# The low-word matmuls of a 64-token rest: 64 rows each, two accumulations on two row halves

## The chip, the core and the metric

The kernel runs on one core of one Trainium2 chip. The metric is device time in microseconds for one execution. Time before: 358.18 us, the median of 3 runs (357.99 to 358.22).

## The reference

Attention with product features, then a gated feed-forward block whose gate mixes over tokens. Batch 4, 4 heads of 32 (so 128 channels), 1088 tokens, d_ff 1024:

```python
q_p, k_p = phi(q), phi(k)                       # outer products of S1 x and S2 x
num = q_p @ (k_p.T @ v);  den = q_p @ sum(k_p) + 1e-6
x = num / den                                    # 1088 x 128 for each batch
h = gelu(x @ w_in);  u, v = h[..., :512], h[..., 512:]
v_n = (v - mean(v)) / sqrt(var(v) + 1e-6) * g_ln
v_s = einsum('ts,bsd->btd', w_sg, v_n) + b_sg[None, :, None]
out = x + (u * v_s) @ w_out
```

The einsum over s is the heavy part: 1088 x 1088 by 1088 x 512 for each of 4 batches.

## The kernel before, in words

**Two words for one number.** Matmul operands are split into a high word in the type fp32r (a rounded float that TensorE takes in one pass) and a low word, the difference to the original. A product is three matmuls: high by high, low by high, high by low.

**The token sum.** For one batch, the class `Gate` computes v_s transposed: 4 blocks `db` of 128 channels (NB) by 3 chunks `ci` of about 362 output tokens (CH; CHL in the last batch: 376, 376, 336). One `db` and `ci` is a *unit*: one accumulation z in a PSUM bank, over 9 tiles `t` of 128 input tokens. 1088 = 8 x 128 + 64, so the last tile, t = 8, holds a rest of 64 tokens. For t = 0 to 7, `spatial_h` issues vh x w_h (L378) and vl x w_h (L380), and `spatial_l` issues vh x w_l (L386). For t = 8, the 64 rest tokens stand twice in the 128 rows: rows 64 to 127 of vn, of w_h and of x repeat rows 0 to 63. `split` writes the high word of the rest into rows 0 to 63 of vh[:, 8] and its low word into rows 64 to 127 (L371), so one matmul at L378 does both products with w_h. The third, at L386, takes all 128 rows too; rows 64 to 127 of w_l[8] are zero (L950), so that the low word drops out. It ends the accumulation (stop).

**Around a unit.** `unit` makes u: three matmuls L395 to L397 into pu and a gelu on ScalarE (L400). After the accumulation, `scale` reads z on VectorE (L407) and frees its bank, and `gate` multiplies by u (L430) and splits the product into gh (ScalarE, L433) and gl (VectorE, L434). The gated chunk goes on a list `pend`; `flush`, at t = 7 of a later unit, issues its three output matmuls into po (L463 to L465). z comes from the pool `psn`, which has two banks; the attention sum pkv (L200) takes its turn there as well.

**Batch 0** is different: block 0 is summed in plain fp32 at L937, 9 tiles by 3 chunks, with t = 8 over 64 rows, and block 1 (`first == 1` in `main`) runs its three chunks side by side, all high words first and then all low words. Blocks 2 and 3 of batch 0, and all blocks of batches 1 to 3, go unit by unit. That makes 45 accumulations with a low-word matmul at t = 8.

**Order of the work.** While `Gate.main` of one batch runs, `tick` issues steps of the next batch's attention and first projections (`Side`, with the hand-tuned due times FIRST and LATER). The head is in a fixed order; after it, a scheduler orders each engine's instructions, and `high_priority` pulls scale, gelu and gate forward.

Of the kernel before, what the change touches and what calls it, by code (L numbers as in the profile page):

```python
# [18 lines left out]
P = 128  # L19
# [69 lines left out]
def tile_kernel(ctx: ExitStack, tc: tile.TileContext, qd, kd, vd, sd, wd, bd, wind, gd, woutd, identd, outd):  # L89
# [84 lines left out]
    class Attention:  # L174
# [69 lines left out]
        def qp2(self, j):  # L244
            ci, p = divmod(j, 2)
            cw = CH[ci][1]
            a, b = (x[:, p, :cw] for x in self.e[ci])
            V.tensor_mul(a, a, b)
            qph, qpl = self.qp[j] = [self.pool([P, 512], "r", f"qp{i}{self.b}_{j}", F32R)[:, :cw] for i in "hl"]
            A.copy(qph, a)  # L250
            G.tensor_sub(qpl, a, f32(qph))

        def q3(self, ci):
            c0, cw = CH[ci]
            den = self.pool([P, 512], "r", f"den{self.b}_{ci}")[:, :cw]
            pn = []
            for p in range(2):
                qp = self.qp.pop(2 * ci + p)
                pd = bank(f"pnd{self.b}_{ci}_{p}")[:, :cw]
                kv = [k[:, P * p : P * p + P] for k in self.kvs]  # L260
                mm(pd, lhsT=kv[0], rhs=qp[0], start=True, stop=False)
                mm(pd, lhsT=kv[1], rhs=qp[0], start=False, stop=False)
                mm(pd, lhsT=kv[0], rhs=qp[1], start=False, stop=True)
                yield
                pn.append(pd)
                do = slice(64 * (1 - p), 64 * (1 - p) + 64)
                A.activation(den[64 * p : 64 * p + 64], pd[do], AF.Identity, bias=eps_t[do], scale=1.0)  # L267
                yield
            x = self.pool([P, 512], "r", f"x{self.b}_{ci}")[:, :cw]
            V.reciprocal(den, den)  # L270
            yield
            for p in range(2):
                r = slice(64 * p, 64 * p + 64)
                V.tensor_mul(x[r], pn[p][r], den[r])
            yield
            cs = slice(c0, c0 + cw)
            xh, xl = self.x
            A.copy(xh[:, cs], x)
            yield
            V.tensor_sub(xl[:, cs], x, f32(xh[:, cs]))  # L280
            if ci == len(CH) - 1:
                for t in self.x:
                    V.tensor_copy(t[:, S:SP], f32(t[:, S - 64 : S]))

    class Gate:
# [68 lines left out]
        def split(self, db, t0, n):  # L354

            if db not in self.parts:
                vh = self.pool([P, NT, P], "vh", f"vh{self.b}_{db}", F32R)
                vl = self.pool([P, NT - 1, P], "vl", f"vl{self.b}_{db}", F32R)
                self.parts[db] = vh, vl
            vh, vl = self.parts[db]  # L360
            ts = slice(t0, t0 + n)
            vs = self.vn[:, :, P * db : P * db + P]
            A.copy(vh[:, ts], vs[:, ts])  # L363
            yield
            last = t0 + n == NT
            ts = slice(t0, t0 + n - last)
            if n > last:
                self.last = V.tensor_sub(vl[:, ts], vs[:, ts], f32(vh[:, ts]))  # L368
            if last:

                self.last = V.tensor_sub(vh[64:128, NT - 1], vs[64:128, NT - 1], f32(vh[64:128, NT - 1]))  # L371

        def spatial_h(self, z, db, ci, t):

            vh, vl = self.parts[db]
            c0, cw = self.ch[ci]
            cs = slice(c0, c0 + cw)
            last = mm(z, lhsT=vh[:, t], rhs=w_h[:, t, cs], start=(t == 0), stop=False)  # L378
            if t < NT - 1:
                last = mm(z, lhsT=vl[:, t], rhs=w_h[:, t, cs], start=False, stop=False)  # L380
            return last

        def spatial_l(self, z, db, ci, t):

            c0, cw = self.ch[ci]
            mm(z, lhsT=self.parts[db][0][:, t], rhs=w_l[t][:, c0 : c0 + cw], start=False, stop=(t == NT - 1))  # L386

        def unit(self, pool, db, ci):

# [47 lines left out]
        def end(self, db, ci):  # L437

            self.final = db, ci
            xh, xl = self.x  # L440
            self.wf = self.pool([P, C], "wf", "wout_f")
            V.tensor_add(self.wf, f32(wout_h[:, db]), f32(wout_l[:, db]))
            self.xs = []
            for c0, cw in self.ch:
                self.xs.append(self.pool([P, 512], "r", f"x_f{c0}")[:, :cw])
                V.tensor_add(self.xs[-1], f32(xh[:, c0 : c0 + cw]), f32(xl[:, c0 : c0 + cw]))

        def out(self, pool, db, ci, gh, gl):
# [28 lines left out]
        def main(self, pool, tick, first, pend, extra=()):  # L477
            extra = list(extra)
            if first == 1:
# [3 lines left out]
                for i in range(2 * NT):  # L483
                    t = i % NT
                    if i in (SPL):
                        run(self.split(2, 3 * SPL.index(i), 3))
                    for ci in range(len(self.ch)):
                        (self.spatial_l if i >= NT else self.spatial_h)(zs[ci], 1, ci, t)
                        if extra and i > XL and i % 2 and ci == 2:
                            extra.pop(0)()  # L490
                        if (i + ci) % 2:
                            tick()
                for ci in range(len(self.ch)):
                    gt = self.scale(pool, zs[ci], 1, ci)
                    u = us.pop() if us else self.unit(pool, 1, ci)
                    pend.append(self.gate(pool, gt, u, 1, ci))
                first = 2
            for db in range(first, NB):
                for ci in range(len(self.ch)):
                    cw = self.ch[ci][1]  # L500
                    u = self.unit(pool, db, ci)
                    z = bank(f"pz{self.b}_{db}_{ci}", "psn", 2)[:, :cw]
                    for t in range(NT):
                        self.spatial_h(z, db, ci, t)
                        self.spatial_l(z, db, ci, t)
                        if db + 1 < NB and ci == 0 and t in (1, 3, 5):
                            run(self.split(db + 1, 3 * (t // 2), 3))

# [4 lines left out]
                            extra.pop(0)()  # L513
                        if t < NT - 1:
                            tick()
                    if (db, ci) == self.final:
                        pend.append(self.gate_final(pool, z, u, db, ci))
                    else:
                        pend.append(self.gate(pool, self.scale(pool, z, db, ci), u, db, ci))
                    tick()  # L520

    class Plan:
# [85 lines left out]
    class Head:  # L608
# [80 lines left out]
        def build(self):  # L689
# [2 lines left out]
            raw_win = [stage([P, DG], "wst", f"win_raw{i}", I64) for i in (1, 0)][::-1]  # L692
            s = stage([P, 16], "ssp", "s_f")
            k = pool([P, SP], "kld", "k0")
            q = [pool([P, 512], "r", f"q0_{c}")[:, : 3 * P] for c in range(3)]
            qp = [pool([P, 3, 3 * P], "vh", f"qp0_{p}") for p in range(2)]

            kps = g.vn[:, 4:NT].rearrange("p t d -> p (t d)")[:, : NT * 2 * P]
# [166 lines left out]
                V.reciprocal(den[c], den[c])  # L865

            def xt1(c):
                xt[c] = pool([P, 512], "r", f"xt0_{c}")[:, : 3 * P]
                V.tensor_tensor(
                    xt[c].rearrange("p (g d) -> p g d", d=D), view(c)[:, :, :D],  # L870
                    den[c].unsqueeze(2).broadcast_to([P, 12, D]), op=ALU.mult,
                )
# [70 lines left out]
                return A.copy(w_h[:, t], w_f[t])  # L943

            def w_lo(t):
                r = slice(0, P if t < NT - 1 else 64)
                w_l[t] = wpool([P, S], "w", f"w_l{t}", F32R)
                if t == NT - 1:

                    G.memset(f32(w_l[t][64:128]), 0.0)  # L950
                V.tensor_sub(w_l[t][r], w_f[t][r], f32(w_h[r, t]))

            for t in range(NT):
                for ci in range(3):
# [143 lines left out]
```

## Time and profile before

| | |
|---|---|
| median of 3 runs | 358.18 us |
| span of the profiled execution | 356.8 us |
| granted TensorE clock, mean | 0.997 |
| L378, high x high | 405 matmuls, mean duration 332 ns |
| L380, low x high | 360 matmuls, mean duration 328 ns |
| L386, high x low | 405 matmuls (45 of them at t = 8), mean duration 329 ns |
| weight loads of these three lines | 188 ns each |

PE is TensorE's matmuls, PEld its weight loads, DVE VectorE, ACT ScalarE, POOL GpSimd. In a timeline row stand the start in us, the time in us, engine, line, operation, output <- inputs, the rows and columns of the weights (128*128), the moving operand (128x362) and the count; in brackets the idle time before it, and what ended it. Durations of matmuls overlap, so the pace is read from start to start.

### The profile page before, as it was taken

How to read it: one execution, taken by the hardware profiler on the slowest of the kernel's cores; microseconds unless marked ns; L12 is line 12 of the kernel's file. 1: busy time of each engine (PE TensorE's matmuls, PEld its weight loads, DVE VectorE, ACT ScalarE, POOL GpSimd, SP SyncE). 2: the span in 40 equal slices, each digit the busy share in tenths (PEclk: the TensorE clock that was granted, in tenths of full speed). 3: DMA queues.
4: the chain of work that ended last, by engine and by line, in shares of the span. 5: the costliest groups of instructions: out<-in, count | busy, mean ns of one | idle time of the engine just before them, and what ended most of it. 6: DMA issues, size and time to landing. Idle time of an engine off the chain costs nothing.

```text
span 356.8 us, 5497 instructions
## 1 busy us (share of the span) xinstructions
PE 348.4 (98%) x2024; PEld 323.1 (91%) x2024; DVE 233.5 (65%) x552; ACT 186.2 (52%) x463; POOL 22.1 (6%) x37
## 2 busy tenths in 40 slices
PE   8999999999999999999999999999999999999995
PEld 7875669898999989999898999999998999999994
DVE  4797899987929359636846766654867656552333
ACT  5475951346394983314558992323368992132120
POOL 0003000131020000022020000021120000000000
PEclk9999999999999999999999999999999999999998
DMA  7993001959200032883000006671000000100001
GB/s 228 396 410 136 2 0 31 215 153 250 71 0 2 1 83 87 224 226 121 2 0 21 3 21 147 189 177 54 0 2 1 2 0 24 42 0 2 0 2 62
DMA packets 18266, 30.19 MB, mean 85 GB/s; under 512 B 1984, under 2 KB 15168, under 8 KB 18240
## 3 DMA queue, kind: packets, MB, share of 16 engines
q1 hardware_dynamic: 18096, 29.76, 28.1%
q8 instruction: 16, 0.26, 0.3%
q10 hardware_dynamic: 144, 0.09, 0.1%
q14 instruction: 10, 0.08, 0.1%
HBM read 20.92 MB, written 8.91 MB: 84 GB/s over the span
## 4 chain that ended last, share of the span: by engine, by line
PE 88%; DVE 5%; ACT 3%; POOL 1%; issue 1%; DMA 1%; DVEq 0%; ACTq 0%
PE pz L378 19%; PE pz L386 19%; PE pz L380 17%; PE pkv L204 3%; PE pu L395 2%; PE pz L937 2%; PE po L465 2%; PE pu L397 2%; PE pu L396 2%; PE po L463 2%; PE po L464 2%; PE pv L299 2%; PE pab L813 2%; PE pk L189 2%; PE pv L300 2%; PE pv L301 2%
## 5 line engine op out<-in xcount | busy, mean ns | idle before, releaser
L378 PE MATMUL pz<-w_h,vh 128*128 128x362 f32 (+3 forms) x405 | 133.7, 332 | 0.0
L386 PE MATMUL pz<-w_l,vh 128*128 128x362 f32 (+3 forms) x405 | 129.4, 329 | 0.0
L380 PE MATMUL pz<-w_h,vl 128*128 128x364 f32 (+3 forms) x360 | 118.1, 328 | 0.0
L378 PEld LDWEIGHTS pz<-w_h,vh 128*128 128x128 f32 x405 | 75.7, 188 | 1.5 <-DVE gt L407 0.6
L386 PEld LDWEIGHTS pz<-w_l,vh 128*128 128x128 f32 x405 | 75.6, 188 | 0.3
L380 PEld LDWEIGHTS pz<-w_h,vl 128*128 128x128 f32 x360 | 67.8, 188 | 0.8
L433 ACT CAST gh<-gt 128x362 fp32r<-128x362 f32 (+3 forms) x47 | 23.1, 495 | 59.0 <-PE po L464 50.5
L407 DVE SCALAR_TENSOR_TENSOR gt<-pz,g_col,b_bc 128x362 f32<-128x362 f32 (+3 forms) x47 | 27.7, 592 | 39.9 <-PE pz L386 39.4
L434 DVE TENSOR_TENSOR gl<-gt,gh 128x362 fp32r<-128x362 f32 (+3 forms) x47 | 24.8, 531 | 15.1 <-ACT gh L433 14.9
L400 ACT ACTIVATE u<-pu 128x362 f32<-128x362 f32 (+3 forms) x48 | 22.4, 471 | 18.1 <-PE pu L397 15.4
L430 DVE TENSOR_TENSOR gt<-gt,u 128x362 f32<-128x362 f32 (+3 forms) x47 | 25.0, 532 | 8.1 <-ACT u L400 7.5
L350 ACT ACTIVATE vn<-vn,nm,rs 128x512 f32<-128x512 f32 x36 | 27.7, 811 | 4.7 <-POOL nm L684 3.9
L270 DVE RECIPROCAL den<-den 128x362 f32<-128x362 f32 (+1 forms) x9 | 21.8, 2418 | 10.0 <-ACT den L267 10.0
L368 DVE TENSOR_TENSOR vl<-vn,vh 128x384 fp32r<-128x384 f32 (+2 forms) x60 | 22.9, 420 | 7.5 <-ACT vh L363 7.3
L363 ACT CAST vh<-vn 128x384 fp32r<-128x384 f32 (+1 forms) x63 | 23.1, 420 | 3.4 <-PE pz L386 3.4
L308 ACT ACTIVATE waste<-vn,mv 128x512 bf16<-128x512 f32 x27 | 19.6, 726 | 0.3
L305 ACT ACTIVATE vn<-pv 128x512 f32<-128x512 f32 x27 | 16.0, 595 | 6.4 <-PE pv L301 6.3
L937 PE MATMUL pz<-w_f,vn 128*128 128x362 f32 (+3 forms) x54 | 18.0, 476 | 0.8 <-ACT vn L350 0.7
L395 PE MATMUL pu<-x_h,win_h 128*128 128x362 f32 (+3 forms) x48 | 16.7, 349 | 0.0
L937 PEld LDWEIGHTS pz<-w_f,vn 128*128 128x128 f32 (+1 forms) x54 | 9.8, 189 | 7.6 <-ACT vn L350 2.4
L463 PE MATMUL po<-gh,wout_h 128*128 128x362 f32 (+3 forms) x47 | 16.0, 341 | 0.0
L396 PE MATMUL pu<-x_h,win_l 128*128 128x362 f32 (+3 forms) x48 | 15.7, 328 | 0.0
(201 smaller groups left out, 530.6 us busy)
## 6 DMA issues: line engine op xcount, KB each, us to landing
w_f<-in_w SPq DMA_DIRECT2D x9, 544.0 KB, 9.8
vx<-in_v SPq DMA_DIRECT2D x8, 288.0 KB, 6.6
k<-in_k SPq DMA_DIRECT2D x3, 576.0 KB, 4.2
e_0d<-ab SPq DMA_DIRECT2D x3, 364.0 KB, 4.0
e_0d<-ab SPq DMA_DIRECT2D x6, 182.0 KB, 5.3
e_0a<-e_0d SPq DMA_DIRECT2D x3, 364.0 KB, 4.7
e_0b<-e_0d SPq DMA_DIRECT2D x3, 364.0 KB, 4.6
q<-in_q SPq DMA_DIRECT2D x6, 181.0 KB, 2.4
```

Of the source, the lines that this page charges most:

```text
L350: A.activation(self.vn[:, t], self.vn[:, t], AF.Identity, bias=self.nm[:, t : t + 1], scale=self.rs[:, t : t + 1])
L363: A.copy(vh[:, ts], vs[:, ts])
L378: last = mm(z, lhsT=vh[:, t], rhs=w_h[:, t, cs], start=(t == 0), stop=False)
L380: last = mm(z, lhsT=vl[:, t], rhs=w_h[:, t, cs], start=False, stop=False)
L386: mm(z, lhsT=self.parts[db][0][:, t], rhs=w_l[t][:, c0 : c0 + cw], start=False, stop=(t == NT - 1))
L395: mm(pu, lhsT=win_h[:, ws], rhs=xh[:, cs], start=True, stop=False)
L407: V.scalar_tensor_tensor(gt, z, g_col[:, db : db + 1], b_bc[:, c0 : c0 + cw], op0=ALU.mult, op1=ALU.add)
L430: V.tensor_mul(gt, gt, u)
L433: A.copy(gh, gt)
L434: V.tensor_sub(gl, gt, f32(gh))
L463: mm(o, lhsT=wout_h[:, db], rhs=gh, start=(db == 0), stop=False)
L937: return mm(zs[ci], lhsT=g.vn[r, t, :P], rhs=w_f[t][r, c0 : c0 + cw], start=(t == 0), stop=(t == NT - 1),)
```

## The change

The t = 8 low-word matmul becomes a matmul over 64 rows, the new function `tail`. It can stand on either row half: on rows 0 to 63 with the high word where it was, or on rows 64 to 127, where w_l[8] now holds its copy (no zeros) and a tenth slice vh[:, 9] holds the high word of the rest in rows 64 to 127, written by one more cast on ScalarE. Units go in pairs. The first unit of a pair is left open without its tail. In the second, after the high matmuls of t = 0, the second's tail is issued on the upper half and right after it the first's on the lower half, which ends the first accumulation; then the first is scaled and gated. The second unit is ended by its L380 (the former L378) at t = 8. In batch 0's block 1, the three tails come one after the other on the halves lower, upper, lower. The pool `r` goes from 512 to 384 columns a tile.

```diff
 def split(...):
-                vh = self.pool([P, NT, P], "vh", f"vh{self.b}_{db}", F32R)
+                vh = self.pool([P, NT + 1, P], "vh", f"vh{self.b}_{db}", F32R)
...
             A.copy(vh[:, ts], vs[:, ts])
-            yield
             last = t0 + n == NT
+            if last:
+                A.copy(vh[64:128, NT], vs[64:128, NT - 1])
+            yield
...
-            last = mm(z, lhsT=vh[:, t], rhs=w_h[:, t, cs], start=(t == 0), stop=False)
+            last = mm(z, lhsT=vh[:, t], rhs=w_h[:, t, cs], start=(t == 0), stop=stop)
...
-            mm(z, lhsT=self.parts[db][0][:, t], rhs=w_l[t][:, c0 : c0 + cw], start=False, stop=(t == NT - 1))
+            mm(z, lhsT=self.parts[db][0][:, t], rhs=w_l[t][:, c0 : c0 + cw], start=False, stop=False)
+
+        def tail(self, z, db, ci, upper, stop):
+
+            c0, cw = self.ch[ci]
+            r = slice(64 * upper, 64 * upper + 64)
+            return mm(
+                z, lhsT=self.parts[db][0][r, NT - 1 + upper], rhs=w_l[NT - 1][r, c0 : c0 + cw],
+                start=False, stop=stop,
+            )
...
-                        (self.spatial_l if i >= NT else self.spatial_h)(zs[ci], 1, ci, t)
+                        if i == 2 * NT - 1:
+                            self.tail(zs[ci], 1, ci, ci == 1, True)
+                        else:
+                            (self.spatial_l if i >= NT else self.spatial_h)(zs[ci], 1, ci, t)
...
                     for t in range(NT):
-                        self.spatial_h(z, db, ci, t)
-                        self.spatial_l(z, db, ci, t)
+                        self.spatial_h(z, db, ci, t, open_ is not None and t == NT - 1)
+                        if t == 0 and open_ is not None:
+                            with tc.issue_after(self.tail(z, db, ci, True, False).ins):
+                                self.tail(*open_[:3], False, True)
+                            pend.append(self.gate(pool, self.scale(pool, *open_[:3]), open_[3], *open_[1:3]))
+                        if t < NT - 1:
+                            self.spatial_l(z, db, ci, t)
...
-                    if (db, ci) == self.final:
-                        pend.append(self.gate_final(pool, z, u, db, ci))
+                    if open_ is None:
+                        open_ = z, db, ci, u
                     else:
-                        pend.append(self.gate(pool, self.scale(pool, z, db, ci), u, db, ci))
+                        open_ = None
+                        if (db, ci) == self.final:
+                            pend.append(self.gate_final(pool, z, u, db, ci))
+                        else:
+                            pend.append(self.gate(pool, self.scale(pool, z, db, ci), u, db, ci))
...
             def w_lo(t):
-                r = slice(0, P if t < NT - 1 else 64)
                 w_l[t] = wpool([P, S], "w", f"w_l{t}", F32R)
-                if t == NT - 1:
-
-                    G.memset(f32(w_l[t][64:128]), 0.0)
-                V.tensor_sub(w_l[t][r], w_f[t][r], f32(w_h[r, t]))
+                V.tensor_sub(w_l[t], w_f[t], f32(w_h[:, t]))
```

The compiled order of TensorE shows the move. In the changed kernel, line numbers shift: L378 and L380 of before are L380 and L382, L386 is L388, L395 to L397 are L406 to L408, and `tail` is L394. In names, pz_2_2 is the accumulation of block 2, chunk 2, and the last figure tells allocations apart; w_l_590 (before) and w_l_591 (after) are the low word of tile t = 8. First batch 0 before, where unit (2, 2) ends and (3, 0) begins:

```order
L378 MATMUL pz_2_2_1083<-w_h,vh_2_696 128x362
L386 MATMUL pz_2_2_1083<-w_l_590,vh_2_696 128x362
L395 MATMUL pu_3_0_1125<-x_h,win_h 128x364
L396 MATMUL pu_3_0_1125<-x_h,win_l 128x364
L397 MATMUL pu_3_0_1125<-x_l,win_h 128x364
L378 MATMUL pz_3_0_1131<-w_h,vh_3_940 128x364
L380 MATMUL pz_3_0_1131<-w_h,vl_3_941 128x364
L386 MATMUL pz_3_0_1131<-w_l_525,vh_3_940 128x364
```

The same place after the change:

```order
L380 MATMUL pz_2_2_1085<-w_h,vh_2_696 128x362
L406 MATMUL pu_3_0_1119<-x_h,win_h 128x364
L407 MATMUL pu_3_0_1119<-x_h,win_l 128x364
L408 MATMUL pu_3_0_1119<-x_l,win_h 128x364
L380 MATMUL pz_3_0_1125<-w_h,vh_3_941 128x364
L382 MATMUL pz_3_0_1125<-w_h,vl_3_942 128x364
L394 MATMUL pz_3_0_1125<-w_l_591,vh_3_941 128x364
L394 MATMUL pz_2_2_1085<-w_l_591,vh_2_696 128x362
L388 MATMUL pz_3_0_1125<-w_l_525,vh_3_941 128x364
```

The two tails stand next to each other, the last of (2, 2) five matmuls later than before, and 128-row matmuls are on both sides of them. (The tails' shape reads 128x364 in this print; it is that of the output.) The second place is in batch 1, where (2, 0) ends and (2, 1) begins. After the change:

```order
L380 MATMUL pz_2_0_1923<-w_h,vh_2_1686 128x364
L380 MATMUL pz_2_1_1975<-w_h,vh_2_1686 128x362
L382 MATMUL pz_2_1_1975<-w_h,vl_2_1687 128x362
L394 MATMUL pz_2_1_1975<-w_l_591,vh_2_1686 128x362
L299 MATMUL pv_0_1896<-win_h,x_h 128x512
L300 MATMUL pv_0_1896<-win_h,x_l 128x512
L301 MATMUL pv_0_1896<-win_l,x_h 128x512
L394 MATMUL pz_2_0_1923<-w_l_591,vh_2_1686 128x364
L388 MATMUL pz_2_1_1975<-w_l_525,vh_2_1686 128x362
```

Here the scheduler put three matmuls of the next batch's projection between the two tails, so each stands alone among 128-row matmuls. The third place is the end of batch 0's block 1, after the change; pk and pkv belong to the next batch's attention:

```order
L388 MATMUL pz_1_1_620<-w_l_589,vh_1_503 128x362
L388 MATMUL pz_1_2_621<-w_l_589,vh_1_503 128x362
L394 MATMUL pz_1_0_619<-w_l_591,vh_1_503 128x364
L189 MATMUL pk_5_738<-sk,k_609 128x128
L394 MATMUL pz_1_1_620<-w_l_591,vh_1_503 128x362
L394 MATMUL pz_1_2_621<-w_l_591,vh_1_503 128x362
L204 MATMUL pkv_778<-vx,kp_0_630 128x128 x2
```

The first of the three tails is alone, and the other two are side by side. In all, the 45 tails stand as 20 adjacent pairs and 5 singles (this one, and two pairs of batch 1 that were drawn apart).

More of the change, by code (lines that the diff above doesn't have):

```diff
@@ L248, in qp2 @@
             V.tensor_mul(a, a, b)
-            qph, qpl = self.qp[j] = [self.pool([P, 512], "r", f"qp{i}{self.b}_{j}", F32R)[:, :cw] for i in "hl"]
+            qph, qpl = self.qp[j] = [self.pool([P, 384], "r", f"qp{i}{self.b}_{j}", F32R)[:, :cw] for i in "hl"]
             A.copy(qph, a)
@@ L254, in q3 @@
             c0, cw = CH[ci]
-            den = self.pool([P, 512], "r", f"den{self.b}_{ci}")[:, :cw]
+            den = self.pool([P, 384], "r", f"den{self.b}_{ci}")[:, :cw]
             pn = []
@@ L268, in q3 @@
                 yield
-            x = self.pool([P, 512], "r", f"x{self.b}_{ci}")[:, :cw]
+            x = self.pool([P, 384], "r", f"x{self.b}_{ci}")[:, :cw]
             V.reciprocal(den, den)
@@ L363, in split @@
             A.copy(vh[:, ts], vs[:, ts])
+            last = t0 + n == NT
+            if last:
+                A.copy(vh[64:128, NT], vs[64:128, NT - 1])
             yield
-            last = t0 + n == NT
             ts = slice(t0, t0 + n - last)
@@ L371, in split, with spatial_h @@
                 self.last = V.tensor_sub(vh[64:128, NT - 1], vs[64:128, NT - 1], f32(vh[64:128, NT - 1]))
-        def spatial_h(self, z, db, ci, t):
+        def spatial_h(self, z, db, ci, t, stop=False):
             vh, vl = self.parts[db]
@@ L444, in end @@
             for c0, cw in self.ch:
-                self.xs.append(self.pool([P, 512], "r", f"x_f{c0}")[:, :cw])
+                self.xs.append(self.pool([P, 384], "r", f"x_f{c0}")[:, :cw])
                 V.tensor_add(self.xs[-1], f32(xh[:, c0 : c0 + cw]), f32(xl[:, c0 : c0 + cw]))
@@ L515, in main @@
                             tick()
-                    if (db, ci) == self.final:
-                        pend.append(self.gate_final(pool, z, u, db, ci))
-                    else:
-                        pend.append(self.gate(pool, self.scale(pool, z, db, ci), u, db, ci))
+                    if open_ is None:
+                        open_ = z, db, ci, u
+                    else:
+                        open_ = None
+                        if (db, ci) == self.final:
+                            pend.append(self.gate_final(pool, z, u, db, ci))
+                        else:
+                            pend.append(self.gate(pool, self.scale(pool, z, db, ci), u, db, ci))
                     tick()
@@ L694, in build @@
             k = pool([P, SP], "kld", "k0")
-            q = [pool([P, 512], "r", f"q0_{c}")[:, : 3 * P] for c in range(3)]
+            q = [pool([P, 384], "r", f"q0_{c}")[:, : 3 * P] for c in range(3)]
             qp = [pool([P, 3, 3 * P], "vh", f"qp0_{p}") for p in range(2)]
@@ L867, in xt1 @@
             def xt1(c):
-                xt[c] = pool([P, 512], "r", f"xt0_{c}")[:, : 3 * P]
+                xt[c] = pool([P, 384], "r", f"xt0_{c}")[:, : 3 * P]
                 V.tensor_tensor(
```

## The prediction

> **What bounds the kernel now.** I read the page's busy table and its chain first, then the engines by stage, then single instructions of TensorE at the one place where the kernel before already uses 64 rows. The busy table and the chain of work that ended last:
>
> ```profile
> span 356.8 us, 5497 instructions
> PE 348.4 (98%) x2024; PEld 323.1 (91%) x2024; DVE 233.5 (65%) x552; ACT 186.2 (52%) x463; POOL 22.1 (6%) x37
> ...
> PE 88%; DVE 5%; ACT 3%; POOL 1%; issue 1%; DMA 1%; DVEq 0%; ACTq 0%
> ```
>
> TensorE carries 88% of the chain; no other engine is over 65% busy. Does that hold in the stage that the change touches, all after 52 us? The table of stretches, whose columns are bounds, length, then the busy time and count of PE, PEld, DVE, ACT and POOL, and clock:
>
> ```profile
> 52.00:130.00 78.00, 77.06 (x458) 72.70 (x457) 59.94 (x124) 43.26 (x121) 7.08 (x7) 1.00 0.31 83
> 130.00:204.00 74.00, 72.96 (x432) 69.38 (x431) 47.15 (x108) 41.65 (x110) 5.70 (x6) 1.00 0.33 92
> 204.00:278.00 74.00, 74.00 (x449) 71.42 (x448) 47.79 (x99) 38.71 (x104) 5.71 (x6) 1.00 0.29 71
> 278.00:357.00 79.00, 74.60 (x446) 73.50 (x444) 37.85 (x100) 29.12 (x70) 0.00 (x0) 0.98 0.04 15
> ```
>
> It does: PE is busy 77.06 of 78, 72.96 of 74 and 74.00 of 74 us, at a granted clock of 1.00. A busy PE may still be a PE that waits, so next the list of waits between 52 and 352 us (total, times, longest), complete for PE:
>
> ```profile
> PE pk L189 <- ACT u L400: 1.1, 2, 0.8
> PE po L458 <- DVE gt L421: 0.3, 1, 0.3
> PE pnd L261 <- ACT u L400: 0.3, 1, 0.3
> PE pv L299 <- ACT u L400: 0.2, 1, 0.2
> ```
>
> That is 1.9 us in 300. So nearly every nanosecond added to or taken from TensorE's stream in this stage goes to the end of the kernel, and the whole question is what the 45 last low-word matmuls cost as 64-row matmuls, against what they cost now. The steady stream, a window of the timeline inside an accumulation:
>
> ```profile
> 179.94 0.32 PE L380 MATMUL pz<-w_h,vl 128*128 128x362 f32 x1
> 180.10 0.33 PE L386 MATMUL pz<-w_l,vh 128*128 128x362 f32 x1
> 180.27 0.33 PE L378 MATMUL pz<-w_h,vh 128*128 128x362 f32 x1
> 180.44 0.32 PE L380 MATMUL pz<-w_h,vl 128*128 128x362 f32 x1
> ```
>
> The durations overlap; what counts is start to start: (180.44 - 179.94) / 3 = 0.167 us a matmul. The weights of the next one are loaded while one runs:
>
> ```profile
> 180.10 0.19 PEld L378 LDWEIGHTS pz<-w_h,vh 128*128 128x128 f32 x1
> 180.27 0.19 PEld L380 LDWEIGHTS pz<-w_h,vl 128*128 128x128 f32 x1
> ```
>
> The load for the matmul of 180.27 starts at 180.10, with the matmul before it. That cover is what makes 0.167 possible.
>
> **What the change does to that stream.** *Entering and leaving a 64-row form.* The accumulations of batch 0, block 0 (L937, plain fp32) end in six 64-row matmuls today, so the trace has one entry and one exit. The entry, PE and PEld:
>
> ```profile
> 48.54 0.47 PE L937 MATMUL pz<-w_f,vn 128*128 128x362 f32 x1
> 48.93 0.18 PEld L937 LDWEIGHTS pz<-w_f,vn 64*128 64x128 f32 x1 [0.51 <-ACT vh L363]
> 49.04 0.19 PEld L937 LDWEIGHTS pz<-w_f,vn 64*128 64x128 f32 x1
> ```
>
> The first 64-row weight load does not start with the matmul of 48.54, as loads do above; it starts 0.39 us later. The trace lays this on ScalarE, but both inputs were ready long before. The activation that wrote this part of vn, and the cast that reads the same w_f:
>
> ```profile
> 44.51 0.80 ACT L350 ACTIVATE vn<-vn,nm,rs 128x512 f32<-128x512 f32 x1
> 46.17 1.10 ACT L943 CAST w_h<-w_f 128x1088 fp32r<-128x1088 f32 x1
> ```
>
> vn was done at 45.31, and w_f had landed by 46.17, for the cast reads it then. And the exit, where the load waits for nothing that the profile shows:
>
> ```profile
> 49.95 0.46 PE L937 MATMUL pz<-w_f,vn 64*128 64x362 f32 x1
> 50.56 0.46 PE L937 MATMUL pz<-w_f,vn 64*128 64x362 f32 x1
> 50.95 0.19 PEld L395 LDWEIGHTS pu<-x_h,win_h 128*128 128x128 f32 x1 [0.51 <-issue]
> 50.96 0.43 PE L395 MATMUL pu<-x_h,win_h 128*128 128x364 f32 x1
> 51.23 0.33 PE L396 MATMUL pu<-x_h,win_l 128*128 128x364 f32 x1
> ```
>
> Again 50.95 - 50.56 = 0.39 from the last matmul of one form to the first load of the other. Between 49.95 and 50.56 lie two steps, 0.305 each, the full pace of these fp32 matmuls. So the load waits 0.39 - 0.305 = 0.085 beyond the last matmul's own step, as if the array had to run empty. Then the matmul waits for its uncovered load: L396 starts 51.23 - 50.96 = 0.27 after L395 where 0.167 is normal, 0.103 more. One change of form costs 0.085 + 0.103 = 0.19 us, one visit to the 64-row form (in and out) 0.38. The Trainium skill has a rule that fits and speaks against this change ("TensorEngine Tiling (Array Packing)", Key Properties): going from one tiling mode to another, and not merely to another tile, makes TensorE drain. It gives no price; the trace agrees that there is one, twice.
>
> *How many visits.* The compiled order of the changed kernel, counted through, has the 45 tails in 20 adjacent pairs and 5 singles: 25 visits. The singles are one at the end of batch 0's block 1 (three tails make one pair and one over) and two pairs of batch 1 between whose halves the scheduler put 128-row matmuls. So 50 changes of form x 0.19 = **+9.4 us** (0.188 unrounded).
>
> *What a pair saves.* Two tails took 2 x 0.167. On different row halves they may run together, but the second's weights are loaded after the first's: the two 64-row loads above start 49.04 - 48.93 = 0.11 apart. So the second matmul starts 0.11 after the first, and the pair saves 0.167 - 0.11 = 0.057; 20 x 0.057 = **-1.1 us**. This overlap is in no row of before, hence bounds: at worst none, and 0 is saved; at best the pair takes one step, 20 x 0.167 = -3.3. I take the middle value because loads are the nearest rows that I have. The Trainium skill ("TensorE: Matmul & The Clock Gate", Part 3, Packing small matmuls) has matmuls on different row groups start about 4 ns apart; by that rule the saving would be 20 x 0.163 = 3.3 and the sum 2.2 us lower. No run shows it yet. A single saves nothing: a matmul of 64 rows steps as one of 128 (the 0.305 above holds for both forms).
>
> *What else moves.* 15 more casts on ScalarE (L366 of the changed kernel, 64 x 128), one fewer memset on GpSimd, and a w_l subtraction over 128 rows instead of 64. The nearest rows for these:
>
> ```profile
> L363 ACT CAST vh<-vn 128x128 fp32r<-128x128 f32 x27 | 6.5, 295 | 0.0
> L951 DVE TENSOR_TENSOR w_l<-w_f,w_h 128x1088 fp32r<-128x1088 f32 x8 | 10.3, 1283 | 0.0
> L951 DVE TENSOR_TENSOR w_l<-w_f,w_h 64x1088 fp32r<-64x1088 f32 x1 | 1.3, 1277 | 0.0
> ```
>
> 15 x 0.295 = 4.4 us on an engine with 171 us idle; the subtraction costs the same for half the rows. The cover is the time between a split and its use in the next block, at least a unit of 26 matmuls x 0.167 = 4.3 us; uncovered, at a batch's first block, one cast would cost 0.3 us, three times. Zero taken. The first unit of each pair now ends its sum after the next unit's first three matmuls, and its gate (L407, L430, L433, L434) starts that much later; queued behind it on VectorE is only the next unit's work, and the output matmuls that need it stand some 18 steps (3 us) behind. Zero taken; what it costs if that fails is a rival below. The three accumulators of the first stage end with two visits (0.76 us) ahead of the matmul that waits for the first of them:
>
> ```profile
> PEld pkv L204 <- DVE gt L407: 0.3, 1, 0.3
> ```
>
> This 0.3 us wait goes: **-0.3**. The other waits of TensorE listed above could shrink as it gets later: 0 to -1.9 us, zero taken, kept for the range. The scheduler also reorders side work: about 1 us either way, judged by the size of the single waits (0.2 to 0.8).
>
> *Sum.* +9.4 - 1.1 - 0.3 = +8.0 us. The profiled execution would go from 356.8 to 364.8. The median of the runs is 358.18, which is 1.4 above that span, so 358.2 + 8.0 = **366.2 us**. Ends of this case: 358.2 + 9.4 + 1 = 368.6 with no overlap in a pair, and 358.2 + 9.4 - 3.3 - 1.9 = 362.4 with full overlap and all waits absorbed.
>
> **Rivals.**
> *A: no price for the change of form.* What the trace shows might belong to the two-pass fp32 matmuls of L937 and not to the one-pass fp32r ones here. Then the pairs save 20 x 0.167 = 3.3 us (1.1 if loads set the distance) and the time is 354.9 us, faster. It decides from the point where a visit costs less than 0.13 us (20 x 0.167 / 25). Against it: the exit of 50.56 leads into an fp32r matmul and pays. That of before has no fp32r row of 64 speaks for leaving it a chance: 9%. The packing page of the Trainium skill named above models a pair as one matmul's time and 4 ns, without any price for getting there; that is this rival.
> *B: only the drain.* If the 64-row weights go into a free half while the 128-row matmul runs, only the 0.085 stays: 50 x 0.085 = 4.25, less 1.1 to 3.3: 359.1 to 361.4 us. Against it: both loads of the trace start after the drain, not before. 7%.
> *C: forms dear, and gates late as well.* A reciprocal on VectorE ahead of a late gate:
>
> ```profile
> L270 DVE RECIPROCAL den<-den 128x362 f32<-128x362 f32 x6 | 14.5, 2416 | 8.2 <-ACT den L267 8.2
> L407 DVE SCALAR_TENSOR_TENSOR gt<-pz,g_col,b_bc 128x362 f32<-128x362 f32 x24 | 14.1, 593 | 16.5 <-PE pz L386 16.3
> ```
>
> 2.42 us, and the gate's four steps 0.6 + 0.5 + 0.5 + 0.5, make 4.5 against 3 us: 1.5 us late, for about half of the 9 reciprocals 6.8 us, 373 us. Against it: the order lets the output matmuls slide back, and no wait of PE for gh is in the list. 4%.
> *D: the tails are not side by side.* The order shows 20 adjacent pairs; only if chip and order differed would all 45 be visits of their own (358.2 + 45 x 0.38 = 375.3). Under 1%, left out.
>
> **The numbers.** The forecast's case has 80%, A 9%, B 7%, C 4%. Its own range is 362.4 to 368.6; I give 361.8 to 369.0, which takes in a little of B's upper end and of other reorderings, and leaves A, most of B, C and the edges of the case itself, about 2 in 10. A measurement of this kernel tells about 0.2% (0.7 us) from no change. Faster by more: A, 0.09. Within: B's lower end, 0.04. Slower by more: 0.87.
>
> **What would show it.** In the changed kernel's trace, the weight load of a pair's first tail starts about 0.25 us after the matmul before it (0.167 + 0.085) instead of with it; the pair's second load 0.11 behind the first; the next 128-row load 0.25 after the second tail; and PE's step across the pair is about 0.33 us longer than before, the same at nearly every pair. If loads of both forms start along with the matmul before them, the forecast is wrong and A holds. If the second tail starts within 0.02 us of the first, the saving is at its upper bound. New waits of PE for gh in the list of waits would be C.

## The result, and the profile after

The changed kernel takes 382.1 us (median of 4 runs, 380.7 to 382.6) against 358.1 us before (4 runs). The ratio is 1.066, with a 95% interval of 1.063 to 1.068: slower by 24 us. The forecast was slower by 8 us, at most 11. The profiled execution took 382.4 us, with a span of 380.2 us.

The page of the changed kernel, with its busy table, the granted clock in 40 slices of 9.5 us, and the chain:

```profile
span 380.2 us, 5512 instructions
PE 364.2 (96%) x2024; PEld 326.9 (86%) x2024; DVE 236.8 (62%) x552; ACT 192.1 (51%) x478; POOL 21.8 (6%) x36
...
PE   8999999999999799999999999499999999999995
...
PEclk9999999999999859999999999669999999999999
...
PE 70%; DVE 8%; ACT 3%; DMA 2%; issue 2%; SPq 1%; DVEq 0%; ACTq 0%
```

Two things are new. TensorE is no longer busy throughout (a 7 and a 4 in its row), and in the slices there its clock is down (8, 5 and 6, 6). Its share of the chain has gone from 88% to 70%. The list of TensorE's waits between 52 and 375 us is headed by these four (the numbers are the total in us, how often, and the longest):

```profile
PE pab L237 <- ACT qt_2h L230: 3.2, 1, 3.2
PE pkv L204 <- DVE kp L148: 1.8, 1, 1.8
PE pz L380 <- ACT vh L363: 1.4, 1, 1.4
PE pz L380 <- DVE kv L214: 1.0, 2, 0.5
```

Before, all waits came to 1.9 us, the longest 0.8. Three of the four are for the next batch's attention, whose steps run beside the gate: qt is a cast of the loaded q, kp goes into the sum pkv, and kv reads that sum and so frees its bank. None of the new ones is for gh, on which rival C rested. The price of the tails themselves can be read from one pair, in the timeline of PE and PEld:

```profile
155.83 0.32 PE L382 MATMUL pz<-w_h,vl 128*128 128x364 f32 x1
156.09 0.43 PE L394 MATMUL pz<-w_l,vh 64*128 64x364 f32 x2
156.44 0.43 PE L388 MATMUL pz<-w_l,vh 128*128 128x364 f32 x1
156.71 0.33 PE L380 MATMUL pz<-w_h,vh 128*128 128x364 f32 x1
...
156.08 0.18 PEld L394 LDWEIGHTS pz<-w_l,vh 64*128 64x128 f32 x2 [0.23 <-issue]
156.44 0.19 PEld L388 LDWEIGHTS pz<-w_l,vh 128*128 128x128 f32 x1 [0.17 <-issue]
```

The first 64-row load starts 0.25 us after the 128-row matmul ahead of it, not with it; the 128-row load 0.35 to 0.36 after the tails; both as forecast in kind. Both loads of the pair, and both matmuls, make one row (x2, 0.18 and 0.43 in all): they run together. From L382 to the second 128-row matmul behind the pair are 156.71 - 155.83 = 0.88 us; without the tails' form, the four steps between these five matmuls would take 4 x 0.167 = 0.67. A pair costs 0.21 us. For 20 pairs, and 5 singles at 0.38, that is 6.2 us of the 24.

The other part begins at the start of batch 1. PE, with the idle time before an instruction in brackets, and below it ScalarE:

```profile
129.31 0.33 PE L408 MATMUL pu<-x_l,win_h 128*128 128x362 f32 x1
130.19 0.49 PE L189 MATMUL pk<-sk,k 128*128 128x128 f32 x2 [0.56 <-ACT u L411]
132.07 0.67 PE L380 MATMUL pz<-w_h,vh 128*128 128x364 f32 x1 [1.38 <-ACT vh L363]
...
132.86 0.51 PE L388 MATMUL pz<-w_l,vh 128*128 128x364 f32 x1
133.16 0.51 PE L380 MATMUL pz<-w_h,vh 128*128 128x364 f32 x1
...
134.21 0.67 PE L394 MATMUL pz<-w_l,vh 64*128 64x362 f32 x1
...
133.85 0.29 ACT L366 CAST vh<-vn 64x128 fp32r<-64x128 f32 x1
```

TensorE idles 0.56 and 1.38 us, and then steps at 0.30 us (132.86 to 133.16) where 0.167 is normal: its clock is at half. The second unit's tail, at 134.21, comes right after the added cast that it needs (133.85 + 0.29 = 134.14), and only then do the second unit's other tiles, t = 1 and on, start. In the kernel before, the time up to 130 us is filled with those tiles (the matmuls of 362 columns are the second unit's):

```profile
128.77 0.33 PE L380 MATMUL pz<-w_h,vl 128*128 128x362 f32 x1
...
129.69 0.41 PE L378 MATMUL pz<-w_h,vh 128*128 128x362 f32 x1
...
130.11 0.32 PE L386 MATMUL pz<-w_l,vh 128*128 128x362 f32 x1
```

### The profile page after: what moved, and what is told of

The parts are those of the page before. It is cut to its first block, busy times and chain, and to the rows that moved or that the text cites. A ratio compares the mean times of both kernels' runs of the same rounds, so it can differ in the third digit from the quotient of the medians.

```text
span 380.2 us, 5512 instructions
## 1 busy us (share of the span) xinstructions
PE 364.2 (96%) x2024; PEld 326.9 (86%) x2024; DVE 236.8 (62%) x552; ACT 192.1 (51%) x478; POOL 21.8 (6%) x36
## 4 chain that ended last, share of the span: by engine, by line
PE 70%; DVE 8%; ACT 3%; DMA 2%; issue 2%; SPq 1%; DVEq 0%; ACTq 0%
PE pz L380 16%; PE pz L388 15%; PE pz L382 14%; PE pkv L204 3%; PE pz L394 2%; PE pu L406 2%; PE po L476 2%; PE po L474 2%; PE pu L407 2%; PE pu L408 2%; PE po L475 2%; PE pv L299 2%; PE pv L300 1%; PE pv L301 1%; DVE den L270 1%
## 5 line engine op out<-in xcount | busy, mean ns | idle before, releaser
L380 PE MATMUL pz<-w_h,vh 128*128 128x362 f32 (+3 forms) x405 | 134.2, 338 | 2.4 <-ACT vh L363 1.4
L382 PE MATMUL pz<-w_h,vl 128*128 128x364 f32 (+3 forms) x360 | 120.4, 334 | 0.0
L388 PE MATMUL pz<-w_l,vh 128*128 128x364 f32 (+3 forms) x360 | 119.9, 343 | 0.0
L380 PEld LDWEIGHTS pz<-w_h,vh 128*128 128x128 f32 x405 | 77.9, 193 | 4.2 <-ACT vh L363 2.1
L388 PEld LDWEIGHTS pz<-w_l,vh 128*128 128x128 f32 x360 | 69.1, 193 | 4.1 <-issue 4.0
L382 PEld LDWEIGHTS pz<-w_h,vl 128*128 128x128 f32 x360 | 69.7, 194 | 0.8 <-issue 0.3
L445 DVE TENSOR_TENSOR gl<-gt,gh 128x362 fp32r<-128x362 f32 (+3 forms) x47 | 25.6, 548 | 28.0 <-ACT gh L444 27.7
L370 DVE TENSOR_TENSOR vl<-vn,vh 128x384 fp32r<-128x384 f32 (+2 forms) x60 | 25.7, 457 | 8.2 <-ACT vh L363 7.9
L363 ACT CAST vh<-vn 128x384 fp32r<-128x384 f32 (+1 forms) x63 | 23.4, 418 | 9.6 <-PE pz L394 8.3
L204 PE MATMUL pkv<-vx,kp 128*128 128x128 f32 x108 | 15.5, 290 | 1.8 <-DVE kp L148 1.8
L406 PE MATMUL pu<-x_h,win_h 128*128 128x362 f32 (+3 forms) x48 | 16.8, 349 | 0.3 <-ACT vn L305 0.3
L204 PEld LDWEIGHTS pkv<-vx,kp 128*128 128x128 f32 x108 | 14.2, 201 | 2.7 <-DVE kp L148 2.3
L148 DVE TENSOR_TENSOR kp<-pk,kb 128x256 f32<-128x256 f32 x27 | 11.0, 422 | 8.9 <-ACT kb L192 7.6
```

Source lines behind the costliest of these rows:

```text
L204: self.summed = mm(self.pkv[:, P * p : P * p + P], lhsT=kp[:, P * p : P * p + P], rhs=vx[:, NT : NT + t + 2 : t + 1] if p else vx[:, t : N ...
L406: mm(pu, lhsT=win_h[:, ws], rhs=xh[:, cs], start=True, stop=False)
L445: V.tensor_sub(gl, gt, f32(gh))
```

## The experiments

Twelve kernels, in three groups. The kernel before, measured beside each group, took 358.5 us (e1, e2, x0, x3), 358.2 (x1, x2 and the two b) and 358.7 (the three f, e4). Two theories stood at first: F, the 64-row form is to blame for all, and P, most of it is the pairing, with two places of its own: the tail that stands third in the second unit's accumulation, and the bank that an open first unit holds while the attention sum pkv needs one.

**e1_pairs_full_rows**: the pairs as they are, without the form.

```diff
-                z, lhsT=self.parts[db][0][r, NT - 1 + upper], rhs=w_l[NT - 1][r, c0 : c0 + cw],
+                z, lhsT=self.parts[db][0][:, NT - 1], rhs=w_l[NT - 1][:, c0 : c0 + cw],
...
-                A.copy(vh[64:128, NT], vs[64:128, NT - 1])
...
+                    G.memset(f32(w_l[t][64:128]), 0.0)
```

> The pairs and their order are kept, but each tail is the old matmul over all 128 rows (the rest's low rows against zeros), so that no change of form is left. Theory P (most of the loss comes from the pairing: an open accumulator holds a PSUM bank and its tail needs the last token tile, TensorE waits at the batch boundaries and its clock drops): only the price of the visits goes, 20 pairs x 0.217 + 5 singles x 0.385 = 6.3 us, so 382.1 - 6.3 = about 376 us, with the waits near 130 and 238 us and two stretches of half clock still there. Theory F (the 64-row form itself is to blame for all of it, also for the waits): about 358 us and no half clock before the end.

Measured: 375.8 us. F falls: without any change of form 17 of the 24 us remain, and so do the waits and the low clock (the first two rows of its list of waits, and a window of it, with the clock 0.53 behind the counts):

```profile
PE pab L237 <- ACT qt_2h L230: 4.9, 1, 4.9
PE pz L378 <- ACT vh L363: 1.4, 1, 1.4
```

```profile
237.00:248.00 11.00, 8.40 (x28) 7.74 (x29) 6.07 (x14) 3.37 (x8) 0.95 (x1) 0.53 0.42 84
```

The wait of 1.4 us for vh is the same without the added cast, so the cast is not its cause. The difference to the changed kernel, 382.1 - 375.8 = 6.3 us, agrees with the 6.2 worked out from the pair's rows as the price of the 25 visits. The agreement is closer than this run can prove: it also lacks the cast, and its wait for qt is longer, 4.9 us against 3.2.

**e2_single_64**: the form without pairs, in the order of before.

```diff
-            mm(z, lhsT=self.parts[db][0][:, t], rhs=w_l[t][:, c0 : c0 + cw], start=False, stop=(t == NT - 1))
+            r = slice(0, P if t < NT - 1 else 64)
+            mm(z, lhsT=self.parts[db][0][r, t], rhs=w_l[t][r, c0 : c0 + cw], start=False, stop=(t == NT - 1))
```

> The kernel before, with each of its 45 tails over 64 rows at its old place and nothing paired; the order of TensorE is unchanged. Theory P with a visit price of 0.385 us (0.085 to drain and 0.105 to load, twice): 358.1 + 45 x 0.385 = 375.4 us, the same extra at every tail, no half clock. Theory F needs about 24 us from 25 visits, 0.95 each: 358.1 + 45 x 0.95 = 401 us. If a change of form were free: 358 us.

Measured: 373.4 us, 14.9 more than before; no low clock until the last microseconds. A visit from its timeline, around the tail that is now in L387:

```profile
318.17 0.33 PE L378 MATMUL pz<-w_h,vh 128*128 128x376 f32 x1
318.43 0.44 PE L387 MATMUL pz<-w_l,vh 64*128 64x376 f32 x1
318.79 0.44 PE L396 MATMUL pu<-x_h,win_h 128*128 128x376 f32 x1
319.07 0.34 PE L397 MATMUL pu<-x_h,win_l 128*128 128x376 f32 x1
319.24 0.33 PE L398 MATMUL pu<-x_l,win_h 128*128 128x376 f32 x1
```

Three steps take 319.07 - 318.17 = 0.90 us; at the 0.17 of 319.07 to 319.24 they would take 0.51: 0.39 a visit. The 45 tails make 43 visits (the three of batch 0's block 1 follow each other), so 14.9 us would be 0.35 each. The trace says more: set against the same matmuls of the kernel before, 42 of the 43 visits lengthen TensorE's stream by 0.38 to 0.40 us and one by 0.26, 16.5 us together, and some 1.6 us come back where short waits and slow steps of before shrink. So the price read from six fp32 matmuls, which step at 0.305 us, holds for the fp32r ones, which step at 0.167, and rivals A and B are out.

**x0_unpaired**, **x1_not_first_two**, **x2_not_third**, **x3_not_block0**: the changed kernel with some or all units taken out of the pairs. One condition differs (in x0, batch 0's block 1 has full tails too):

```diff
+                        alone = open_ is None and not (CONDITION)
                         if t < NT - 1:
                             self.spatial_l(z, db, ci, t)
+                        elif alone:
+                            self.tail(z, db, ci, None, True)
...
-                    if open_ is None:
+                    if open_ is None and not alone:
```

A tail called with None for its half takes all 128 rows. CONDITION is what keeps a unit in its pair:

```
x0  False
x1  self.b == 0 or (db, ci) not in ((0, 0), (0, 1))
x2  (db, ci) not in ((0, 2), (NB - 1, 2))
x3  db > 0 and (db, ci) != (NB - 1, 2)
```

> The changed kernel with no pair at all and every tail over 128 rows at its old place (the extra cast, the copy of the low word in the lower rows and the smaller pool stay; the tails then add the product low by low of the rest, which the kernel before leaves out). Both theories: 358.1 us within 1, as the cast and the subtraction are off the path. If the cast on ScalarE delays the batch boundaries: 360 or more.

Measured: 359.9 us, ratio 1.0045 (1.0030 to 1.0060): 1.4 us over before, a little more than expected. The cast and the other small parts are not quite free; which of them costs this was not tried.

> The changed kernel, but in batches 1 to 3 block 0's three units stay unpaired (tails over 128 rows, which add the product low by low of the rest), and so does the last unit of a batch; the pairs begin with block 1. 16 pairs and one single visit stay. Theory P: no bank is held across the attention sum pkv and no tail stands ahead of the first units' other tiles, so the waits and the half clock go; 358.1 + 16 x 0.217 + 0.385 = 362 us. Theory F: 17 of 25 visits, so 358.1 + 24 x 17/25 = 374 us.

Measured: 367.3 us. The clock stays up and the long waits are gone, as P has it, but 9 us over before are more than the visits' 3.9. Of the other 5, about 2 are in its list of waits (3.8 us against 1.9 before; new is one for qpl, from GpSimd, 1.3 us in five), and what x0 costs is in it too; the rest was not followed.

> The changed kernel, but in batches 1 to 3 the first two units are unpaired (tails over 128 rows, which add the product low by low of the rest); the pair of the third unit with block 1's first, which spans the attention sum pkv, stays. 19 pairs and one single visit: 358.1 + 19 x 0.217 + 0.385 = 362.6 us without waits. Theory P, two separate waits (a tail ahead of the other tiles at a batch's start, and a bank held across pkv): the wait of 1.4 us near 131 us and the half clock after it go, the long waits near 238 to 247 us and their half clock stay, about 12 us with the clock: 373 to 377 us. If the first pair caused the later waits as well: about 363 to 367 us.

Measured: 367.4 us, next to the 363 to 367 of the other case, and here P fell in part. Taking the first pair alone out of each batch removed the wait at 131 us and also the long ones near 240. The pair that spans pkv is still there, and TensorE waits 0.9 us for kv. The clock is 1.00 from 120 to 150 and from 225 to 260 us.

> The changed kernel, but in batches 1 to 3 the third unit (and the last of a batch) is unpaired, with its tail over 128 rows (which adds the product low by low of the rest); the first two units stay a pair, and no pair is open while pkv is summed. Theory P: the long waits at pkv go, the wait near 131 us for the last token tiles and the half clock behind it stay: 18 pairs and 3 single visits, 5.1 us, + 1.4 + 4 for the clock + 3 for reordering: 370 to 373 us, one half-clock stretch near 131 us. If the open pair at pkv is not the cause: 378 us or more with the waits near 240 us still there.

Measured: 375.7 us, worse than expected, with the clock low at both places (windows of it):

```profile
133.00:141.00 8.00, 7.29 (x24) 5.96 (x25) 4.23 (x10) 3.96 (x10) 0.00 (x0) 0.57 0.37 92
235.00:254.00 19.00, 16.81 (x90) 15.09 (x89) 11.74 (x24) 7.09 (x17) 3.13 (x3) 0.91 0.66 178
```

TensorE still waits near 240, 1.6 us for kp; its wait for qt is down to 0.3. The edit does not keep every pair away from pkv: in the compiled order the pair of block 1's first two units takes the place of the one taken out. Its first unit has its last full matmul at 240.03 us, the last matmuls of pkv run from 244.75, and the second unit starts at 246.43, when kv has freed the bank. It is the same in x3. So neither tests a sum without an open pair. Beyond the price of the visits, some 18 us remain in the changed kernel, 12 here and 5 in x1: the larger part goes with the first pair of a batch. What the open bank adds is read from the timelines below, at f1.

**b_after** and **b_before**: a third bank for z and pkv, taken from the pool ps.

```diff
-    def bank(name, tag="ps", bufs=3):
+    def bank(name, tag="ps", bufs=2):
...
-                self.pkv = bank(f"pkv{self.b}", "psn", 2)[:, : 2 * P]
+                self.pkv = bank(f"pkv{self.b}", "psn", 3)[:, : 2 * P]
...
-                    z = bank(f"pz{self.b}_{db}_{ci}", "psn", 2)[:, :cw]
+                    z = bank(f"pz{self.b}_{db}_{ci}", "psn", 3)[:, :cw]
```

> The changed kernel with a third bank in the pool psn and one fewer in the pool ps (2 instead of 3), so that two open accumulators and pkv fit at once; to be read against b_before. Theory P: block 1's first unit no longer waits for pkv, and the difference to b_before is the form's 6.3 us and the wait at the batch's start, 9 to 14 us. If the bank is not what the unit waits for: the difference stays about 24 us.

> The kernel before with three banks in psn and two in ps, the control for b_after. Taking a bank from the pool of pu, pk, pv and pab can only add waits, as psn had enough: 358 to 366 us.

Measured: 382.6 and 376.6 us. The control is itself 18 us slower, far outside what was expected of it, with waits of its own for vh (3.5 us) and x_h (3.1 us). The difference of 6.0 is about the visits' price, but with such a control the pair settles little about the bank. In both traces the clock is 1.00 from 225 to 260 us, and there is no wait for qt or kp.

**f2_tail_late** and **f4_late_full_rows**: theory T, formed on x1 and x2. T says that a tail needs the last token tile, and that where it stands third it bars the second unit's other tiles. In batches 1 to 3, only the place of the first pair's tails moves, from after t = 0 of the second unit to after its t = 7, and with it the first unit's scale and gate, which follow its tail (f4 does the same to e1, without the form).

```diff
+                        at = NT - 2 if self.b and (db, ci) == (0, 1) else 0
                         self.spatial_h(z, db, ci, t, open_ is not None and t == NT - 1)
-                        if t == 0 and open_ is not None:
+                        if t == at and open_ is not None:
```

> The changed kernel, but in batches 1 to 3 the first pair's two tails stand after the second unit's t = 7 instead of after its t = 0; nothing else differs, the units stay paired. 22 pairs and 1 single visit, 5.2 us. Theory T (a tail needs the last token tile, and standing third in its accumulation it bars the second unit's other tiles, with which TensorE used to cover the wait for that tile; the later waits follow from it): no wait near 131 us, no half clock, the load of q back in its place: 358.2 + 5.2 + 3 to 5 for reordering = 366 to 369 us. If it is the open accumulator as such, wherever its tail stands: 378 to 383 us.

Measured: 368.0 us, inside the 366 to 369 of T. Windows of the changed kernel and then of f2 at the start of batch 1, with the clock behind the counts:

```profile
129.00:133.00 4.00, 2.06 (x8) 1.52 (x9) 1.56 (x9) 3.26 (x8) 0.00 (x0) 0.77 0.80 170
133.00:141.00 8.00, 8.00 (x25) 6.57 (x23) 4.24 (x10) 3.53 (x9) 0.00 (x0) 0.50 0.38 103
```

```profile
129.00:133.00 4.00, 3.22 (x22) 2.84 (x20) 2.06 (x10) 2.83 (x8) 0.00 (x0) 1.00 0.49 128
133.00:141.00 8.00, 7.82 (x47) 6.68 (x47) 6.03 (x16) 5.21 (x15) 0.00 (x0) 1.00 0.52 125
```

In these 12 us TensorE gets through 33 matmuls in the one and 69 in the other: 36 x 0.167 = some 6 us. The second place is in batch 2, the changed kernel first again:

```profile
237.00:247.00 10.00, 4.82 (x20) 3.86 (x18) 3.09 (x7) 2.96 (x7) 2.81 (x3) 0.67 0.70 183
247.00:254.00 7.00, 6.68 (x21) 5.96 (x22) 5.15 (x12) 2.13 (x5) 0.00 (x0) 0.50 0.11 14
```

```profile
237.00:247.00 10.00, 9.41 (x54) 8.64 (x53) 6.46 (x14) 3.41 (x8) 1.88 (x2) 1.00 0.41 107
247.00:254.00 7.00, 7.00 (x43) 6.59 (x42) 3.71 (x8) 2.14 (x5) 0.00 (x0) 1.00 0.52 140
```

Here it is 41 matmuls against 97, 56 x 0.167 = some 9 us. Two tails a batch in another place, and 14 us come back, the larger part of them far behind the place of the first loss.

> As f2_tail_late, but with tails over all 128 rows (the rest's low rows against zeros), so without any change of form. Theory T: f2_tail_late less 5.2 us, 361 to 364 us; the pairing then costs no more than what the new order of the side work costs. If the form causes waits beyond its own price: 359 us or less.

Measured: 362.5 us, ratio 1.011 (1.008 to 1.014). f2 less f4 gives the visits' price a second time, 5.5 us (5.2 expected; f4 also lacks the added cast). f4 shows that pairs cost 3.9 us over before even without a change of form and without the early tail of a batch's first pair. Its list has 4.5 us of waits against 1.9; new are 1.3 for qpl and 0.9 for kv, the bank of pkv.

**f1_two_q**: the load of q's third chunk. In the changed kernel's batch 2 it is issued at 236.53 us, behind a transfer of the spread, which sends the product ab through device memory to repeat its rows; before, at 209.86 (rows of SP's queue, after and before):

```profile
235.84 0.64 SPq L169 DMA_DIRECT2D e_1a<-e_1d  x1
236.53 0.55 SPq L225 DMA_DIRECT2D q<-in_q  x1
```

```profile
209.86 0.33 SPq L225 DMA_DIRECT2D q<-in_q  x1
```

```diff
-    side = Pool(sp, 1, r=6, kp=3, kb=2, qld=1, ...)
+    side = Pool(sp, 1, r=6, kp=3, kb=2, qld=2, ...)
```

> The changed kernel with two buffers instead of one for the loaded q, so that the load of q's third chunk need not wait for the first to be consumed; in the compiled order of SP it then stands ahead of the spread's transfers again. If that load, queued behind the transfers, is what makes TensorE idle for 3.2 us at 238 us (theory Q): that wait and the half clock after it go, the wait near 131 us stays: 370 to 375 us. If the load is late only because everything before it is late: 380 to 383 us, with the idle time put down to another wait.

Measured: 384.5 us, above both cases. As a remedy it fails. Its windows:

```profile
123.00:154.00 31.00, 25.07 (x89) 20.45 (x90) 14.46 (x53) 21.04 (x59) 0.00 (x0) 0.73 0.21 50
154.00:237.00 83.00, 82.18 (x484) 76.71 (x483) 53.43 (x119) 47.70 (x128) 5.79 (x6) 1.00 0.24 68
```

From 154 us on TensorE is busy at full clock (1.00 from 237 to 262 as well), and the long wait for qt is gone; but the new order brought waits of 5.3 us (for x_h) and 3.7 us (for vh) before 154. In f2 the load is in its old place with one buffer.

Why the late load costs so much in the changed kernel is read from three rows of its PE: the last full matmul of the third unit, the one that waits for qt, and the first of the next unit:

```profile
235.21 0.33 PE L380 MATMUL pz<-w_h,vh 128*128 128x362 f32 x1
...
241.23 0.67 PE L237 MATMUL pab<-qt_2h,sk_h 128*128 128x362 f32 x1 [3.19 <-ACT qt_2h L230]
...
247.32 0.67 PE L380 MATMUL pz<-w_h,vh 128*128 128x364 f32 x1 [0.52 <-DVE kv L214]
```

For 12 us no matmul of an accumulation z runs. The pool psn has two banks: the open third unit holds one, pkv the other, and the last matmuls of pkv (from 244.73 us) stand in TensorE's order behind the one that waits for qt. The next unit gets its bank when kv has read pkv. In f2 a unit is open across pkv too, but the load is early, and the same stretch is 5 us long (230.85 to 235.81) and filled with other matmuls. In x2 the load is as late as here (235.53), but the third unit is closed and its bank free; a unit of 25 matmuls runs from 236.04, and TensorE waits 0.3 us for qt. So the loss in batch 2 takes both, the late load and the open unit. The late load goes with the early tail in the changed kernel, e1 and x2; how the scheduler comes to it was not followed.

**e4_same_half**: both tails of a pair on the lower half.

```diff
-                            with tc.issue_after(self.tail(z, db, ci, True, False).ins):
+                            with tc.issue_after(self.tail(z, db, ci, False, False).ins):
```

> The changed kernel with both tails of every pair on the lower row half, one after the other, so that they can't run together. If the two halves do run together in the changed kernel (their starts are 2 ns apart in its trace): 21 pairs x 0.167 us more, 382.1 + 3.5 - 0.5 (one pair that was drawn apart stands together here) = 385 us. If the starts in the trace only look so: 382 us.

Measured: 384.3 us. The total moves by 2.2 and is clouded by the waits, which are there too; one pair at the same place in both traces is clearer, e4 first, then the changed kernel:

```profile
336.22 0.32 PE L382 MATMUL pz<-w_h,vl 128*128 128x336 f32 x1
336.47 0.58 PE L394 MATMUL pz<-w_l,vh 64*128 64x336 f32 x2
336.99 0.42 PE L388 MATMUL pz<-w_l,vh 128*128 128x336 f32 x1
337.24 0.32 PE L380 MATMUL pz<-w_h,vh 128*128 128x336 f32 x1
```

```profile
336.30 0.32 PE L382 MATMUL pz<-w_h,vl 128*128 128x336 f32 x1
336.55 0.43 PE L394 MATMUL pz<-w_l,vh 64*128 64x336 f32 x2
336.91 0.42 PE L388 MATMUL pz<-w_l,vh 128*128 128x336 f32 x1
337.17 0.32 PE L380 MATMUL pz<-w_h,vh 128*128 128x336 f32 x1
```

1.02 us against 0.87: the pair on two halves saves 0.15 us, a whole step at 336 columns (336.07 to 336.22 in e4), so the two really run together. In e4 the second load of that pair starts 0.11 us after the first, at 336.47:

```profile
336.58 0.19 PEld L394 LDWEIGHTS pz<-w_l,vh 64*128 64x128 f32 x1
```

## Why the prediction was wrong

The direction and the mechanism that it named were right; the time lies 13 us above the top of the range, for a mechanism that it did not have. Its steps:

- *A change of form costs 0.19 us, a visit 0.38.* Right: 0.38 to 0.40 in e2 at all visits but one, and 6.3 us (e1) and 5.5 us (f2 less f4) for all visits together.
- *A pair saves 0.057 us, because the loads follow each other.* Wrong in size: the 0.11 us between loads came from two loads on the same row half, and e4 has it there too; on two halves both loads start together, and the pair saves its upper bound, about one step. The sum for the form should have been +9.4 - 3.3 = 6.1, not 8.3. The Trainium skill's figure of 4 ns between starts ("TensorE: Matmul & The Clock Gate", Part 3, Packing small matmuls) was nearer; the trace agrees, as both starts fall in one row at 156.09 and lie 3 to 4 ns apart in every pair.
- *What else moves: zero for the added cast, zero for the late end of a first unit.* This is the step that failed. It asked who waits for the first unit's gate, and not what the second unit's own tail waits for. A tail needs the last token tile. Third in its accumulation, it bars the other tiles of that unit, and at the start of batch 1 those were TensorE's cover while ScalarE finished the last tiles. The prediction even named the place ("uncovered, at a batch's first block, one cast would cost 0.3 us, three times") and priced only the cast there, not the cover that was gone. e1 and f4 differ in nothing but the place of the first pairs' tails and of what follows them: 375.8 - 362.5 = 13 us. At the start of batch 1 the changed kernel falls some 6 us behind f2. Part of that is the clock: it does 25 matmuls in 133 to 141 us at a step of some 0.30 us instead of 0.167, which alone is 25 x 0.13 = 3.3 us. The larger part, some 9 us between 237 and 254, is the late end of a first unit itself: open across pkv, it holds the second bank of psn, and with the load of q late no matmul of an accumulation z runs for 12 us, and the clock is at half again. That goes with the early tails too, for f2, f4 and x1, where the open unit stays and the load is early, do not have it; why the scheduler puts the load late stays open.
- *The scheduler reorders side work: about 1 us either way.* Too small, as far as f4's 3.9 us come from it: it has neither visits nor the early tail of a first pair, and 2.6 us more in its list of waits than before.
- *TensorE's waits could only shrink as it gets later.* Right where the order stays (e2 gets some 1.6 us back), of the wrong sign in the changed kernel, for the reason above.
- *Rivals.* A and B are out by e2, C by the list of waits, D as forecast. None had the early tail or the clock. One chance does not fit its sum: 0.04 for a time within 0.7 us of before cannot come from B, whose lower end is 359.1, 0.9 us above it.

Put together, as steps from one measured kernel to the next: 6.3 (visits and the cast, after to e1) + 13.2 (early tails of the first pairs, e1 to f4) + 3.9 (the rest of the pairing, f4 to before) = 23.4 of the 24 us; the rest lies in the spread of before between the groups (358.1 to 358.7). Open are why the load of q comes late, and the parts of the 3.9 us and of x0's 1.4 us. No version tried beats the kernel before: a pair gains one step of 0.167 us and pays 0.38 for the visit.

## What to carry to other kernels

Before packing two half-height matmuls side by side, look in the trace for a place where the form changes: a visit cost more than twice what a pair saved here, so several pairs would have to share one visit (by these prices at least three; no run tried it). When an operation is moved forward within an accumulation, ask first what it needs, then what stands behind it in that accumulation: everything behind it inherits its wait, and what used to cover that wait is gone. And an accumulation that is left open holds its bank: look who else needs one before it closes. A short wait can also halve TensorE's clock for many microseconds, as it did here in some places and not in others, so look at the granted clock around every new wait.

## What the runs showed of the hardware

- In the changed kernel TensorE ran at half clock (0.50 in 133 to 141 us) though its longest idle time there was 1.38 us; it had been busy 2.06 of 4 us (129 to 133). The Trainium skill ("TensorE: Matmul & The Clock Gate", Why this matters for your kernels) warns of idle gaps over about 3 us; here less was enough, and the measurement decides. In the kernel before, idle times of up to 0.78 us left the clock at 1.00. The length of one idle time does not decide it: in b_after TensorE idled 2.30 us until 124.53, was busy 1.70 of 4 us (121 to 125), and its clock stayed at 1.00. Nor does it fix how long the half clock lasts: behind the same two waits of 0.56 and 1.38 us it lasted 10.2 us in the changed kernel and 3.4 in e1. What decides was not found.
- Weight loads for the two row halves start together (0.18 us for both), while on one half they start 0.11 us apart and their matmuls go one after the other (0.58 us for the pair of matmuls in e4, 0.43 on two halves).
